# A load that waits for a memset: SyncE issues the second load of wq behind half of GpSimd's zeros

## The chip, the core and the metric

The kernel runs on one core of one Trainium2 chip. The metric is the device time of one execution in microseconds (us); before the change the median of 3 runs is 218.84 us (218.81 to 218.87). Where a profile is read, its times come from one further execution taken with the profiler, and are counted from the start of its span.

## The reference, cut to what matters

One decoding step for two tokens. Attention over the last 4096 positions of a cache and a dense layer with Mish work on the same input, and a sigmoid gate mixes them:

```python
g = sigmoid((x * gate_w).sum(-1, keepdims=True))          # x: 2 x 1 x 512
q = (x @ wq)                                               # 512 x 4096: 32 heads of 128
scores = einsum(q, k[last 4096]) * 128 ** -0.5             # 8 kv heads, each for 4 query heads
a = (softmax(scores) @ v[last 4096]) @ wo                  # 4096 x 512
h = x @ w1 + b1                                            # 512 x 1792
b = (h * tanh(softplus(h))) @ w2                           # 1792 x 512
out = g * a + (1 - g) * b
```

All of it is float32. The weights and the part of the cache that is read are some 91 MB, and each byte is used for only two tokens.

## The kernel before, in words

**Loads.** All large inputs pass through three rotating buffers of 128 partitions x 64 KB (the pool `stream`, lines 61 and 70 to 76). SyncE (SP) issues nearly all loads; its DMAs share one queue, which is spread over 16 DMA engines, so there are 16 rings that each work off their share of a load. The order of issue on SP is: `wq` in two pieces (line 74, called from line 78), the small inputs `sm` (line 80: x, the gate's weights, the bias), eight loads `kv` of 8 MB each, one kv head's keys and values (line 74, called from line 296), `w12` (w1, a part of wo, a part of w2), then the rest of w1, wo and w2 (lines 320, 333, 337). The first piece of `wq`, `in_wqh`, has 2048 columns (HEAD, 1 MB: 8 KB in each partition); the second, `in_wqt`, has the other 14336 (7 MB: 56 KB in each partition). The first two `kv` loads find a buffer free; every later one waits until TensorE is done with the buffer that it takes.

**Work at the start.** GpSimd (POOL) builds an identity matrix and from it small masks (`fold`, `key`, lines 91 to 98), writes ones and zeros (`ones`, `x32`, `qz`, `padded`: lines 103, 106, 109, 112), and when `sm` has landed copies x into `x32` (line 107). `qz`, 128 x 1152, is the tile for the queries: zeros everywhere but where line 155 later puts the transposed queries of each head, so that a matmul of line 163 can take a block of it as weights. ScalarE waits with its first instruction, an activation table load, until the first load has landed (lines 85 to 88). TensorE multiplies x with wq (line 143), so its first instruction needs the first piece of `wq` and `x32`.

**Then**, for each of the 8 kv heads: scores (line 163), maximum, exponential, transposes, values (line 187). Last come w1 (line 258), wo (line 348) and w2 (line 358), the copy of the result (line 391) and the store (line 392).

A scheduler sets the order on each engine. It places an instruction by its own estimates, and what stands on one engine in the program's text is not always the order in which that engine runs it; `keep_in_program_order` (also called `pin`) marks instructions that it leaves in the order of the text.

Of the kernel before, what the change touches and what calls it, by code (L numbers as in the profile page):

```python
# [17 lines left out]
HKV = 8  # L18
# [38 lines left out]
def decode_kernel(ctx: ExitStack, tc: tile.TileContext, res, stored, small, wqh, wqt, kv_in, w12, wo, w2, *rest):  # L57
    *parts, before, behind, out = rest
    nc = tc.nc
# [8 lines left out]
    loads = []  # L68

    def load(name, *parts):  # L70
        t = stream.tile([P, 2 * CHUNK], F32, tag="s", name=name)
        x = 0
        for cols, src in parts:
            loads.append(nc.sync.dma_start(t[:, x : x + cols], src))  # L74
            x += cols
        return t

    wq_t = load("wq", (HEAD, wqh[:, :HEAD]), (2 * CHUNK - HEAD, wqt[:, : 2 * CHUNK - HEAD]))
    sm = const.tile([P, SMALL], F32, name="sm")
    loads.append(nc.sync.dma_start(sm, small))  # L80
    xT = sm[:, : (DC + SLOTS) * B].rearrange("p (c b) -> p c b", b=B)
    gw = sm[:, (DC + SLOTS) * B : (DC + SLOTS) * B + DC]
    b1 = sm[:, (DC + SLOTS) * B + DC :]
# [4 lines left out]
                      reason="ScalarE begins behind the first load")  # L88
# [17 lines left out]
    nc.gpsimd.memset(x32, 0.0)  # L106
    nc.gpsimd.tensor_copy(x32[:, :, ::RS], xT)  # L107
    qz = const.tile([P, HKV, BN * (Q + REP)], F32, name="qz")
    nc.gpsimd.memset(qz, 0.0)
    sizes = (HQ * Q, CUTS[1] * Q, (FC - CUTS[1]) * WIDE, WIDE)  # L110
    padded = const.tile([P, sum(sizes)], F32, name="padded")
    nc.gpsimd.memset(padded, 0.0)
# [182 lines left out]
    for kv in range(HKV):  # L295
        t = load(f"kv{kv}", (2 * CHUNK, kv_in[kv][:, : 2 * CHUNK]))
        p = scores(kv, t[:, :CHUNK])
        ms = tops() if kv == HKV - 1 else None
        pT = turned(kv, p)
        values(kv, pT, t[:, CHUNK:], 0, 1)  # L300
        if kv == HKV - 1:
            kf, kl = factors(ms)
        values(kv, pT, t[:, CHUNK:], 1, 2)
        if kv == HKV - 1:
            r = shares(kl)
        values(kv, pT, t[:, CHUNK:], 2, NT)
    w12_t = load("w12", (AHEAD + CUTS[1] * D, w12))

    def flat(src, cuts, size):
# [4 lines left out]
    x = (WO[-1] - WO[0]) * REP * D  # L314
# [16 lines left out]
    x = 0  # L331
# [3 lines left out]
    x = AHEAD + CUTS[1] * D  # L335
# [31 lines left out]
    first = WO[0] * REP  # L367
# [19 lines left out]
    for ld in loads[-8:]:  # L387
        tc.add_manual_dep(landed.ins, ld.ins.name,
                          mybir.DependencyInfo(mybir.DependencyClass.Sync, mybir.DependencyReason.DATA),
                          reason="SyncE sees the last loads land ahead of the store")  # L390
# [5 lines left out]
                      reason="the store reads the copy")  # L396
# [72 lines left out]
```

## Time and profile before

| | before |
|---|---|
| median of 3 runs | 218.84 us |
| the profiled execution: its own time | 218.95 us |
| the profiled execution: span of its trace | 217.1 us |
| DMA moved, mean over the span | 91.38 MB, 421 GB/s |
| busy: PE, DVE, ACT, POOL | 52%, 10%, 7%, 5% of the span |
| first instruction on PE | 23.12 us |

The span runs from the first instruction in the trace to the last; the 1.85 us by which the execution's own time is longer lie outside it. In the rows a line such as "L74" is a line of the kernel, "SPq" is SyncE issuing DMAs, and names like `wq<-in_wqt` are the tile written and the source. Time after a bar or in brackets as "idle before" is that of the engine just ahead of the instruction, with what ended it.

### The profile page before, as it was taken

What the parts mean: (1) busy time and instruction counts of PE and PEld (TensorE: products, weight loads), DVE (VectorE), ACT (ScalarE), POOL (GpSimd) and SP (SyncE); (2) the same over time, 40 slices, a digit from 0 to 9 for tenths busy, and PEclk for the clock granted to TensorE, in tenths of its full rate; (3) what the DMA queues carried; (4) which work ended last, traced back from release to release, by engine and by line L of the source; (5) the groups of instructions that cost most, each with busy time, mean ns of one, the idle gap of its engine ahead of it and who ended that gap; (6) DMA issues with size and microseconds to landing.
All of it is one profiled execution on the core that took longest, in us unless ns stands there. A gap on an engine that the chain in (4) does not pass through costs nothing.

```text
span 217.1 us, 1858 instructions
## 1 busy us (share of the span) xinstructions
PE 113.3 (52%) x826; PEld 34.5 (16%) x826; DVE 21.5 (10%) x32; ACT 15.4 (7%) x34; POOL 11.4 (5%) x34
## 2 busy tenths in 40 slices
PE   0000797367055609533770753287066608759995
PEld 0000312112011102101120210012011101213342
DVE  0000000010001320100105010010501001250100
ACT  0200001011002000200010020002002000301001
POOL 8000000000000000000000000000000230100300
PEclk9999999889859975996797699679958957999699
DMA  9798998999989998999999999999999999999894
GB/s 362 338 507 351 546 411 386 399 522 423 399 386 519 426 411 386 495 447 399 399 483 450 399 411 447 483 399 411 450 471 399 423 447 430 430 383 468 377 410 159
DMA packets 2752, 91.38 MB, mean 421 GB/s; under 512 B 566, under 2 KB 646, under 8 KB 954
## 3 DMA queue, kind: packets, MB, share of 16 engines
q1 hardware_dynamic: 2602, 91.24, 97.6%
q8 instruction: 6, 0.10, 0.2%
q0 software_dynamic: 144, 0.05, 0.1%
HBM read 91.24 MB, written 0.04 MB: 421 GB/s over the span
## 4 chain that ended last, share of the span: by engine, by line
DMA 78%; PE 15%; ACT 2%; SPq 2%; DVE 1%; issue 1%; POOL 1%; ACTq 0%
DMA kv<-in_kv 61%; DMA w<-in_w 17%; PE sc L163 8%; PE o L187 5%; ACT p L168 1%; PE fin L358 1%; DVE mx L166 1%; SPq L320 1%; PE pp L175 1%; ACT pT L176 1%; POOL wo L316 1%; SPq L333 0%; SPq L74 0%; SPq L80 0%; DVE res L391 0%
## 5 line engine op out<-in xcount | busy, mean ns | idle before, releaser
L163 PE MATMUL sc<-kv,qz 128*32 128x512 f32 x256 | 43.3, 839 | 54.7 <-DMA kv<-in_kv 54.7
L187 PE MATMUL o<-kv,pT 128*32 128x512 f32 x256 | 29.5, 596 | 5.8 <-ACT pT L176 5.8
L163 PEld LDWEIGHTS sc<-kv,qz 128*32 128x32 f32 x256 | 9.7, 149 | 87.7 <-DMA kv<-in_kv 61.3
L143 PE MATMUL qp<-wq,x 128*32 128x512 f32 x64 | 11.4, 760 | 23.1 <-POOL x L107 23.1
L166 DVE TENSOR_REDUCE mx<-sc 128x1 f32<-128x512 f32 x8 | 5.5, 692 | 112.3 <-PE sc L163 112.3
L168 ACT ACTIVATE p<-sc,mx 128x512 f32<-128x512 f32 x8 | 5.5, 687 | 131.2 <-DVE mx L166 131.2
L175 PE MATMUL pp<-ident,p 128*128 128x128 f32 x32 | 5.2, 286 | 12.1 <-ACT p L168 12.1
L187 PEld LDWEIGHTS o<-kv,pT 128*32 128x32 f32 x256 | 7.3, 109 | 20.9 <-issue 13.2
L316 POOL MEMSET wo<- 128x1536 f32 x1 | 1.4, 1377 | 144.4 <-PE o L187 144.4
L197 DVE TENSOR_REDUCE od<-om 128x256 f32<-128x1024 f32 x4 | 7.6, 1898 | 0.1
L143 PEld LDWEIGHTS qp<-wq,x 128*32 128x32 f32 x64 | 2.4, 134 | 28.7 <-POOL x L107 23.1
L348 PE MATMUL acc<-wo,padded 128*32 128x512 f32 x56 | 6.9, 593 | 0.0
L194 DVE TENSOR_TENSOR om<-o,pick 128x1024 f32<-128x1024 f32 x4 | 4.9, 1225 | 19.3 <-PE o L187 19.3
L175 PEld LDWEIGHTS pp<-ident,p 128*128 128x128 f32 x32 | 3.4, 140 | 18.6 <-ACT p L168 18.6
L176 ACT COPY pT<-pp 128x512 f32<-128x512 f32 x8 | 4.7, 585 | 6.2 <-PE pp L175 6.2
L258 PE MATMUL hp<-w,x 128*32 128x512 f32 (+1 forms) x30 | 3.6, 540 | 2.5 <-DMA w<-in_w 2.5
L348 PE MATMUL acc<-w,padded 128*32 128x512 f32 x22 | 4.3, 896 | 0.4 <-DVE padded L241 0.4
L348 PEld LDWEIGHTS acc<-wo,padded 128*32 128x32 f32 x56 | 2.5, 109 | 3.5 <-issue 2.5
L258 PE MATMUL hp<-wo,x 128*32 128x512 f32 x6 | 2.7, 592 | 0.0
L132 DVE RECIPROCAL g<-g 128x2 f32<-128x2 f32 x1 | 0.2, 165 | 22.4 <-POOL g L131 22.4
L358 PE MATMUL fin<-w,padded 128*32 128x128 f32 x56 | 2.1, 277 | 0.4 <-DMA w<-in_w 0.4
L149 PE MATMUL qt<-ident,qs 128*128 128x128 f32 x8 | 1.3, 286 | 1.4 <-ACT qs L146 1.4
(71 smaller groups left out, 35.8 us busy)
## 6 DMA issues: line engine op xcount, KB each, us to landing
wq<-in_wqt SPq DMA_DIRECT2D x1, 7168.0 KB, 21.5
w<-in_w SPq DMA_DIRECT2D x1, 6144.0 KB, 41.3
wo<-in_wo SPq DMA_DIRECT2D x1, 5120.0 KB, 29.6
wo<-in_wo SPq DMA_DIRECT2D x1, 2048.0 KB, 34.1
wq<-in_wqh SPq DMA_DIRECT2D x1, 1024.0 KB, 4.9
w<-in_w SPq DMA_DIRECT2D x1, 1024.0 KB, 36.0
w<-in_w SPq DMA_DIRECT2D x1, 512.0 KB, 35.4
w<-in_w SPq DMA_DIRECT2D x1, 256.0 KB, 21.1
```

Of the source, the lines that this page charges most:

```text
L143: nc.tensor.matmul(qp[Q * k : Q * k + Q, :], x32[:, c, :], w[:, c, k, :], start=(c == 0), stop=(c == DC - 1))
L163: nc.tensor.matmul(sc[Q * j : Q * j + Q, :], qz[:, kv, m * Q : m * Q + Q], t[:, (m * NJ + j) * 512 : (m * NJ + j + 1) * 512], start=(m == ...
L166: nc.vector.tensor_reduce(mx[:, kv : kv + 1], sc, axis=AX.X, op=ALU.max, negate=True)
L168: nc.scalar.activation(p, sc, AF.Exp, bias=mx[:, kv : kv + 1], accum_out=ls[:, kv : kv + 1])
L175: pin(nc.tensor.transpose(pp[:, c, :], p[:, c * P : (c + 1) * P], ident))
L176: nc.scalar.copy(pT, pp)
L187: pin(nc.tensor.matmul(o[Q * j : Q * j + Q], pT[:, c, Q * j : Q * j + Q], t[:, (c * NJ + j) * 512 : (c * NJ + j + 1) * 512], start=(c == 0 ...
L194: nc.vector.tensor_tensor(ov, pair[0].rearrange("p k (m d) -> p k m d", m=BN), pick[:, None, :, None].to_broadcast([P, 2, BN, DH]), op=ALU ...
L197: nc.vector.tensor_reduce(od[:, kv - 1 : kv + 1], ov.rearrange("p k m d -> p k d m"), axis=AX.X, op=ALU.add)
L258: nc.tensor.matmul(hp[Q * j : Q * j + Q, :n], x32[:, c, :], w[:, :n], start=(c == 0), stop=(c == (DC + SLOTS if j in away else DC) - 1))
L348: return nc.tensor.matmul(acc[Q * j : Q * j + Q, :], lhsT, rhs, start=(n_col[j] == 1), stop=(n_col[j] == n))
L358: nc.tensor.matmul(fin[Q * j : Q * j + Q, :], lhsT[:, y : y + Q], rhs[:, j * P : (j + 1) * P], start=(done[0] == 0), stop=(done[0] == n_fi ...
```

## The change

Three things change in the text. The loads of `wq`, `kv` and `sm` are marked to stay in program order. The memset of `qz` becomes two, each of half the heads (128 x 576). And SyncE's issue of `loads[1]`, which is `in_wqt`, the second piece of `wq`, depends on the first of these two memsets: a semaphore from GpSimd. `DependencyReason.DATA` is only the kind of the entry; the load reads nothing that the memset writes.

```diff
         for cols, src in parts:
-            loads.append(nc.sync.dma_start(t[:, x : x + cols], src))
+            loads.append(tc.keep_in_program_order(nc.sync.dma_start(t[:, x : x + cols], src)))
             x += cols
...
-    loads.append(nc.sync.dma_start(sm, small))
+    loads.append(tc.keep_in_program_order(nc.sync.dma_start(sm, small)))
...
     qz = const.tile([P, HKV, BN * (Q + REP)], F32, name="qz")
-    nc.gpsimd.memset(qz, 0.0)
+    half = nc.gpsimd.memset(qz[:, : HKV // 2], 0.0)
+    tc.add_manual_dep(loads[1].ins, half.ins.name,
+                      mybir.DependencyInfo(mybir.DependencyClass.Sync, mybir.DependencyReason.DATA),
+                      reason="the first load has the queues for itself at first")
+    nc.gpsimd.memset(qz[:, HKV // 2 :], 0.0)
     sizes = (HQ * Q, CUTS[1] * Q, (FC - CUTS[1]) * WIDE, WIDE)
```

Line numbers behind the change are 4 higher. On SyncE, at the program's start, the DMAs stood so (tile, source, shape; a number behind a name is that of the buffer, and brackets name the engine whose semaphore the instruction waits for):

```order
L74 DMA wq<-in_wqh 128x2048
L74 DMA wq<-in_wqt 128x14336
L80 DMA sm<-in_small 128x32
L74 DMA kv_170<-in_kv 128x16384
L74 DMA kv_216<-in_kv 128x16384
```

And now, in the same place:

```order
L74 DMA wq<-in_wqh 128x2048
L74 DMA wq<-in_wqt 128x14336 [waits Pool_49]
L80 DMA sm<-in_small 128x32
L74 DMA kv_171<-in_kv 128x16384
L74 DMA kv_217<-in_kv 128x16384
```

The order is the same; the second DMA has got a wait for GpSimd, and the three behind it stand behind that wait. On GpSimd, from the zeros of `x32` on, the order was:

```order
L106 MEMSET x_94 128x224
L93 TENSOR_TENSOR fold<-ident 128x32 [waits Pool_49]
L109 MEMSET qz 128x1152
L95 TENSOR_TENSOR fold<-fold,ident 128x32 [waits Pool_49]
L112 MEMSET padded 128x1744
L95 TENSOR_TENSOR fold<-fold,ident 128x32 [waits Pool_49]
L98 TENSOR_TENSOR key<-fold 128x8 [waits Pool_49]
L117 COPY padded<-fold 128x2
```

And now:

```order
L106 MEMSET x_94 128x224
L93 TENSOR_TENSOR fold<-ident 128x32 [waits Pool_49]
L109 MEMSET qz 128x576
L95 TENSOR_TENSOR fold<-fold,ident 128x32 [waits Pool_49]
L113 MEMSET qz 128x576
L95 TENSOR_TENSOR fold<-fold,ident 128x32 [waits Pool_49]
L116 MEMSET padded 128x1744
L98 TENSOR_TENSOR key<-fold 128x8 [waits Pool_49]
L121 COPY padded<-fold 128x2 [waits Pool_49]
```

The first half stands where the whole memset stood, the second half behind the next addition of `fold`, and the zeros of `padded` have moved behind the second of those additions. Every other engine has the same instructions in the same order as before.

## Prediction

> **What bounds the kernel now.** I read the page first, its row of DMA queues and its chain of work that ended last:
>
> ```profile
> q1 hardware_dynamic: 2602, 91.24, 97.6%
> DMA 78%; PE 15%; ACT 2%; SPq 2%; DVE 1%; issue 1%; POOL 1%; ACTq 0%
> ```
>
> The queue that carries SyncE's loads keeps its 16 rings busy for 97.6% of the span, and 78% of the chain is DMA. So the time is that of 91 MB through 16 rings, plus a stretch ahead of the first byte and one behind the last. An edit to the order of issue can matter in two ways only: by what it does to the rings' throughput, and by a stretch in which a ring has nothing to do. Both are looked for at the start, so next the timeline, its SP and POOL rows of the first microseconds (start, duration, engine, line), with the first row of PE:
>
> ```profile
> 0.73 0.39 SPq L74 DMA_DIRECT2D wq<-in_wqh  x1
> 1.17 0.41 SPq L74 DMA_DIRECT2D wq<-in_wqt  x1
> 1.35 0.27 POOL L106 MEMSET x<- 128x224 f32 x1
> 1.62 0.43 SPq L80 DMA_DIRECT2D sm<-in_small  x1
> 1.79 1.05 POOL L109 MEMSET qz<- 128x1152 f32 x1
> 2.10 1.29 SPq L74 DMA_DIRECT2D kv<-in_kv  x2
> 3.00 1.54 POOL L112 MEMSET padded<- 128x1744 f32 x1
> 22.86 0.21 POOL L107 COPY x<-sm 128x14 f32<-128x14 f32 x1 [17.70 <-DMA sm<-in_small]
> 23.12 1.92 PE L143 MATMUL qp<-wq,x 128*32 128x512 f32 x2 [23.12 <-POOL x L107]
> ```
>
> SyncE issues five loads without a pause, from 0.73 to 3.39 us. TensorE starts only at 23.12, since `sm` sits in the rings behind all of `wq`; nobody but ScalarE's table load uses the first piece early. Third, the DMA view of the window 0 to 6 us, 40 slices of 0.15 us:
>
> ```profile
> GB/s 0 0 0 0 0 0 0 0 0 0 0 382 55 0 164 218 218 218 109 546 273 492 382 437 437 437 437 437 437 382 1475 382 983 2294 1529 382 0 0 0 0
> ```
>
> A packet is evidently counted whole where it starts (2294 GB/s is over five times the mean of 421), which helps here: the pieces can be told apart. Slice 12 (1.65 to 1.80) holds the first packets, 0.92 to 1.07 us after the issue at 0.73. From 3.45 on the rate is even. The jump at slice 31 (4.50 to 4.65) is the first of the far larger packets of `in_wqt`, and the last of them start in slice 36 (5.25 to 5.40). So each ring goes over from the first piece to the second at some point between 4.50 and 5.40, and what it needs of the second piece before that is only that it be queued.
>
> The last stretch, by windows (length, busy time of five engines, granted clock, DMA share, GB/s), and the chain's last pieces:
>
> ```profile
> 212.50:213.00 0.50, 0.09 (x7) 0.10 (x8) 0.00 (x0) 0.40 (x1) 0.00 (x0) 1.00 0.97 393
> 213.00:213.50 0.50, 0.50 (x21) 0.50 (x25) 0.00 (x0) 0.19 (x1) 0.00 (x0) 1.00 0.76 303
> 213.50:214.00 0.50, 0.50 (x28) 0.46 (x19) 0.00 (x0) 0.00 (x0) 0.00 (x0) 1.00 0.63 242
> 214.00:214.40 0.40, 0.40 (x22) 0.31 (x16) 0.00 (x0) 0.00 (x0) 0.00 (x0) 1.00 0.15 56
> ...
> 176.77 36.03 DMA w<-in_w
> 212.80 0.14 issue
> 212.93 2.26 PE fin L358 x64
> ```
>
> The rings do not end together: the DMA share falls from 0.97 to 0.15 over the 1.4 us before 214.4. What the start gives or takes reaches the end only on the rings that are last there.
>
> **The change part by part.** The time is worked out against the profiled execution: span 217.1 us and 1.85 us around it, 218.95 us in all, 0.11 us above the median of the three runs, 218.84.
>
> *When the second load is issued.* The first half is 576 elements in each partition. The rows for 224 and 1152 elements (0.27 and 1.05 us) give 0.84 ns for an element, so the half takes 0.27 + 352 x 0.00084 = 0.57 us. It starts where the whole one did, at 1.79, and ends at 2.36. How fast SyncE reacts to GpSimd shows later in the chain, where a load waits for a memset in the same way:
>
> ```profile
> 172.22 1.39 POOL wo L316
> 173.61 0.02 issue
> 173.62 0.89 SPq L320
> ```
>
> So 0.02 us more: the second load is issued at 2.38 instead of 1.17, which is 1.21 us later. Queued behind the wait on SyncE are `sm` (1.62 to about 2.83) and two `kv` (2.10 and on to about 3.31 and on, ending near 4.60). Nobody waits for these: in the rings they lie behind `wq`, which has landed only here (KB, us from issue to landing):
>
> ```profile
> wq<-in_wqt SPq DMA_DIRECT2D x1, 7168.0 KB, 21.5
> wq<-in_wqh SPq DMA_DIRECT2D x1, 1024.0 KB, 4.9
> ```
>
> that is at 1.17 + 21.5 = 22.7 us, 18 us after the last delayed issue. With that cover gone each microsecond of delay would cost a microsecond.
>
> *Does a ring run dry?* The second piece's first packets are ready 0.92 to 1.07 us behind the issue, as for the first piece: at 3.30 to 3.45. For the slowest ring I have a bound only: the first load is at 546 GB/s in slice 20, which ends at 3.00, so by then the rings have their work, 2.27 us after the issue. That gives 4.65 at the latest. Needed are the packets between 4.50 and 5.40. On the likely value there is over 1 us of room; on the bound the earliest ring waits 0.15 us and one in the middle none. I take 0, with 0.15 as the end on the side of a loss; it is nearer to 0, since a ring slow to get its first piece is also the one that is done with it late.
>
> The Trainium skill, "DMA: Bandwidth & Descriptors", section "Rules for kernel authors", says to issue a DMA early so that its fixed setup lies beside other work, and this change does the contrary. By it alone the 1.21 us would be a loss. Here the row of slices leaves 1 us of setup covered by the 2.9 us and more between the first packets and the first change-over, so the trace supports no loss as long as that cover holds.
>
> *What the first load can gain.* From 1.65 to 3.45 the twelve slices sum to 3057, times 0.15 us: 459 KB. The window behind them shows what the same load does once it runs:
>
> ```profile
> 3.45:4.50 1.05, 0.00 (x0) 0.00 (x0) 0.00 (x0) 0.00 (x0) 1.05 (x1) 1.00 1.02 429
> ```
>
> At 429 GB/s these bytes take 1.07 of the 1.80 us, so the slow start costs 0.73 us, and that is the most that the change can bring. The least is 0, if the slowness is that of a first access, or of the rings' own start. For a gain speaks that the slow slices, 1.80 to 2.85, are those in which SyncE pushes the second load, `sm` and the first `kv`. Against it: the second `kv` is issued up to 3.39, while the four slices from 2.85 to 3.45 already average 423. And the one later place where several loads are issued beside a full stream, six DMAs of SyncE and three of GpSimd from 173.6 to 177.3, shows no loss against the window behind it:
>
> ```profile
> 173.60:177.30 3.70, 0.00 (x0) 0.00 (x0) 0.00 (x0) 0.00 (x0) 1.86 (x3) 0.63 1.03 443
> 177.30:185.00 7.70, 5.23 (x33) 1.24 (x33) 0.69 (x1) 0.52 (x1) 0.00 (x0) 0.73 0.96 412
> ```
>
> That also prices the four moved issues, which now fall into the first load's steady stretch: 443 against 412 says nothing is lost. I take 0 for the gain as well, as this later row is a direct view of issues beside a stream, and keep 0.73 as the other end.
>
> The Trainium skill, "Perfetto Trace Analysis", section "DMA Instruction — HWDGE (DVE, Sync)", has the issuing sequencer hold the descriptor generator for itself until all descriptors of its DMA are made, and only then go on. By it the first load's descriptors are complete at 0.73 + 0.39 = 1.12, ahead of the second issue at 1.17; there would be nothing to disturb and the gain would be 0. The trace has the two issues apart in that way, and does not show the descriptors.
>
> *GpSimd.* Two halves take 2 x 0.57 = 1.14 us instead of 1.05, so 0.09 us more. GpSimd then idles 17.70 us until `sm` lands; this cover hides it, and without it the cost would be 0.09. The moved zeros of `padded` and the additions of `fold` lie under the same cover. Marking loads to stay in order changes nothing on SyncE.
>
> The sum is 0 + 0 + 0: 218.95 for an execution like the profiled one, and 218.8 as a median.
>
> **The rivals.** *The first load does start faster, and the whole stream with it.* Then the slices from 1.80 to 2.85 fill up. Half of the 0.73 us, since the first access itself cannot be free, gives 218.84 − 0.37 = 218.5, all of it 218.1. Against a gain in full: the windows at the end show a last ring alone for a while; rings that gain unevenly bring only what the last one gains, down to nothing.
>
> *The rings run dry between the two pieces: slower.* The place is the change-over, 4.50 to 5.40. It decides once SyncE issues the second load later than 4.50 − 1.07 = 3.43 us with the likely setup, or later than 2.23 with the longest. GpSimd's durations are the uncertain piece: should the half take as long as the whole did, 1.05 us, the issue is at 2.86, and with the longest setup the packets are there at 5.13, so the earliest ring stands still for 0.63 us. If that is one that ends last, the time is 218.84 + 0.63 = 219.5; with a ring that changes over midway, at 4.95, 0.18: 219.0. A price in between is 219.3. It needs the long end of both, hence unlikely.
>
> **How the numbers follow.** About 0.2%, 0.44 us, is what a measurement of this kernel can tell from no change. No change that can be told: chance 0.50, at 218.8, its own range 218.4 to 219.2. A faster start: 0.35, between 218.1 and 218.7, four fifths of it below 218.40. Dry rings: 0.15, between 219.0 and 219.5, most of it beyond 219.28. Faster by over 0.2% then has 0.28, within 0.2% 0.60, slower 0.12. The range 218.1 to 219.2 takes in the first two cases and the lower half of the third.
>
> **What would show it.** Right: `in_wqt` issued near 2.38; slow slices up to 2.85 as before; the large packets starting in 4.50 to 5.40; `sm` landing and PE's first row near 23.1; the same fall of the DMA share around 214. If the slices behind 1.80 fill up and the large packets start earlier than 4.50, with PE's first row earlier by as much, the second case has come about. Zeros in the slices between 4.4 and 5.6 with PE's first row later are the third. PE's first row shifted but the end not, or the reverse, would say that my single line from start to end is wrong.

## The result, and the profile after

| | before | after |
|---|---|---|
| median | 218.82 us (4 runs, 218.78 to 218.87) | 219.78 us (4 runs, 219.66 to 220.37) |
| ratio after/before | | 1.0049, 95% interval 1.003 to 1.0067 |
| the profiled execution: its time, span | 218.95, 217.1 us | 219.66, 217.8 us |

The change makes the kernel 0.96 us slower, outside the range of the prediction (218.1 to 219.2) and on the side to which I had given 0.12. The profiled executions differ by 0.71 us, 0.7 of it in the span.

The timeline's start (start, duration, engine, line) went as worked out: the half memset takes 0.57 us, and the second load is issued at 2.39 instead of 1.17:

```profile
0.73 0.39 SPq L74 DMA_DIRECT2D wq<-in_wqh  x1
1.79 0.57 POOL L109 MEMSET qz<- 128x576 f32 x1
2.39 0.33 SPq L74 DMA_DIRECT2D wq<-in_wqt  x1
2.76 0.43 SPq L80 DMA_DIRECT2D sm<-in_small  x1
3.24 0.91 SPq L74 DMA_DIRECT2D kv<-in_kv  x2
23.38 0.20 POOL L107 COPY x<-sm 128x14 f32<-128x14 f32 x1 [18.31 <-DMA sm<-in_small]
```

`sm`, which lies behind all of `wq` in the rings, is used at 23.38 instead of 22.86, so half a microsecond is gone by then. The DMA view of 0 to 6 us, slices of 0.15 us, looks for it around the first load:

```profile
GB/s 0 0 0 0 0 0 0 0 0 0 0 437 164 0 0 273 109 164 546 328 492 328 492 273 546 328 492 382 492 328 492 983 3168 1529 382 382 0 0 0 0
```

The slow slices from 1.80 to 2.70 are still there. From 1.65 to 3.45 the slices sum to 3333 instead of 3057, 41 KB more, and the window behind them has lost 24 KB of that again:

```profile
3.45:4.50 1.05, 0.00 (x0) 0.00 (x0) 0.05 (x1) 0.00 (x0) 1.05 (x1) 1.00 0.97 406
```

So the first load gains 17 KB by 4.50, or 0.04 us. The large packets of the second load start from 4.65 to 5.40, and no slice between is empty: in this view the rings do not run dry. What has become slow is the second load's own packets. The view of 0 to 12 us (slices of 0.3 us) shows where, before and then after:

```profile
GB/s 0 0 0 0 0 191 27 191 218 328 382 410 437 437 410 928 1639 956 0 0 0 0 382 1720 573 382 0 0 0 382 1147 1147 382 0 0 0 382 956 1338 382
```

```profile
GB/s 0 0 0 0 0 218 82 137 137 437 410 382 437 437 410 737 2349 382 0 0 0 0 0 1529 765 382 382 0 0 0 382 1911 191 573 0 0 0 382 1911 191
```

Each hump is the moment at which the rings start one further packet of 56 KB. Before, the humps start in slices 16, 23, 30 and 37, seven slices or 2.1 us apart. After, the second one starts in slice 24 and drags on to slice 27, and the third starts in 31: some first packets take 0.3 us longer and more. From the third hump on the distance is seven slices again.

The traces also keep every single packet with its start and its length, and these records give the sizes. On a ring the next packet starts as the last one ends, so the rings can be told apart. A packet of 56 KB usually takes 2.12 us. The second load's first packet takes longer, as a mean over the 16 rings by 0.07 us in before and by 0.28 us in after (at most by 0.35 and 0.79). The second packet takes 0.01 and 0.08 us longer, and from the third on it is 0.02 us at most. One ring of after also stands idle for 0.18 us, until 2.90 us behind the issue. The rings then end the second load 0.28 us later on average (22.26 instead of 21.98) and the last of them 0.49 us later (22.82 instead of 22.33), which is the half microsecond by which `sm` is late.

The rate of a longer window is no measure of this, since its edge can cut a hump. Up to 20.00 us it is 420 GB/s in before and 401 in after; up to 21.00 us it is 412 in both (before and after in turn; last columns: DMA share, GB/s):

```profile
5.40:20.00 14.60, 0.00 (x0) 0.00 (x0) 0.00 (x0) 1.28 (x1) 0.00 (x0) 1.00 0.97 420
5.40:20.00 14.60, 0.00 (x0) 0.00 (x0) 0.00 (x0) 1.28 (x1) 0.00 (x0) 1.00 0.93 401
5.40:21.00 15.60, 0.00 (x0) 0.00 (x0) 0.00 (x0) 1.28 (x1) 0.00 (x0) 1.00 0.95 412
5.40:21.00 15.60, 0.00 (x0) 0.00 (x0) 0.00 (x0) 1.28 (x1) 0.00 (x0) 1.00 0.96 412
```

The end follows, by the last pieces of the chain and the windows of after:

```profile
176.09 37.38 DMA w<-in_w
213.48 0.14 issue
213.61 2.29 PE fin L362 x64
```

```profile
213.50:214.00 0.50, 0.39 (x16) 0.42 (x20) 0.00 (x0) 0.14 (x1) 0.00 (x0) 1.00 0.64 254
214.00:214.40 0.40, 0.40 (x24) 0.40 (x17) 0.00 (x0) 0.00 (x0) 0.00 (x0) 1.00 0.37 143
214.40:215.00 0.60, 0.60 (x28) 0.45 (x23) 0.00 (x0) 0.00 (x0) 0.00 (x0) 1.00 0.16 61
```

The last wait for w2 ends at 213.48 instead of 212.80, and the rings are busy up to 215 where they had ended by 214.4. By the packet records, 64 short packets mark the ends of the last four loads on the 16 rings; their mean is 0.20 us later than in before, and the last of them 0.72 us later (215.08 instead of 214.36). So the mean lateness of the rings is only a part of the loss, and the rest lies on the rings that end last. How it gathers on them is not shown.

### The profile page after: what moved, and what is told of

It reads as the page before. It is cut to its first block, busy times and chain, and to the rows that moved or that the text cites. A ratio compares the mean times of both kernels' runs of the same rounds, so it can differ in the third digit from the quotient of the medians.

```text
span 217.8 us, 1859 instructions
## 1 busy us (share of the span) xinstructions
PE 118.0 (54%) x826; PEld 35.4 (16%) x826; DVE 21.6 (10%) x32; ACT 15.5 (7%) x34; POOL 11.4 (5%) x35
## 4 chain that ended last, share of the span: by engine, by line
DMA 77%; PE 16%; ACT 2%; SPq 2%; POOL 1%; DVE 1%; issue 1%; ACTq 0%; POOLq 0%
DMA kv<-in_kv 60%; DMA w<-in_w 17%; PE sc L167 8%; PE o L191 6%; ACT p L172 1%; PE fin L362 1%; DVE mx L170 1%; SPq L324 1%; PE pp L179 1%; ACT pT L180 1%; POOL wo L320 1%; SPq L337 0%; POOL qz L109 0%; SPq L80 0%; DVE res L395 0%
## 5 line engine op out<-in xcount | busy, mean ns | idle before, releaser
L167 PE MATMUL sc<-kv,qz 128*32 128x512 f32 x256 | 45.5, 877 | 51.0 <-DMA kv<-in_kv 51.0
L191 PE MATMUL o<-kv,pT 128*32 128x512 f32 x256 | 31.1, 622 | 5.8 <-ACT pT L180 5.8
L147 PE MATMUL qp<-wq,x 128*32 128x512 f32 x64 | 11.9, 794 | 23.6 <-POOL x L107 23.6
L167 PEld LDWEIGHTS sc<-kv,qz 128*32 128x32 f32 x256 | 10.2, 153 | 85.3 <-DMA kv<-in_kv 57.6
```

The lines of the kernel that those rows point to most:

```text
L147: nc.tensor.matmul(qp[Q * k : Q * k + Q, :], x32[:, c, :], w[:, c, k, :], start=(c == 0), stop=(c == DC - 1))
L167: nc.tensor.matmul(sc[Q * j : Q * j + Q, :], qz[:, kv, m * Q : m * Q + Q], t[:, (m * NJ + j) * 512 : (m * NJ + j + 1) * 512], start=(m == ...
L191: pin(nc.tensor.matmul(o[Q * j : Q * j + Q], pT[:, c, Q * j : Q * j + Q], t[:, (c * NJ + j) * 512 : (c * NJ + j + 1) * 512], start=(c == 0 ...
```

## Experiments

They ran on several chips. Each is compared with the kernel before on its own chip, and "loss" below is the difference of these two medians. "Issue" is that of the second load on SyncE. "Lead" is from there to the middle of the change-over to the second load, 4.95 us with HEAD 2048, near 6.45 with HEAD 3072 and near 7.6 with HEAD 4096. "Long by" is read from the packet records of the profiled execution: by how much the second load's first packet, as a mean over the 16 rings, takes longer than the load's packets usually do (2.12 us for 56 KB, 1.97 for the 52 KB of HEAD 3072, 1.82 for the 48 KB of HEAD 4096). In before it is 0.07 us.

| run | issue, us | lead, us | median, us | loss, us | ratio, 95% interval | long by, us |
|---|---|---|---|---|---|---|
| split_only | 1.18 | 3.8 | 218.89 | 0.01 | 0.9997 to 1.0016 | 0.00 |
| wait_x32 | 1.66 | 3.3 | 218.88 | 0.00 | 0.9995 to 1.0014 | 0.01 |
| wait_sum0 | 1.87 | 3.1 | 218.93 | 0.09 | 0.9999 to 1.0018 | 0.07 |
| after_again, after_third | 2.38, 2.39 | 2.6 | 219.82, 219.69 | 0.96, 0.80 | 1.0039 to 1.0066, 1.0031 to 1.0055 | 0.48, 0.23 |
| wait_sum1 | 2.60 | 2.4 | 219.58 | 0.74 | 1.0023 to 1.0049 | 0.30 |
| wait_whole | 2.87 | 2.1 | 219.45 | 0.58 | 1.0017 to 1.0036 | 0.16 |
| wait_second_half, second_half_again | 3.11 | 1.8 | 218.98, 218.94 | 0.10, 0.05 | 1.0001 to 1.002, 0.9995 to 1.0012 | 0.16, 0.12 |
| wait_padded | 4.81 | 0.1 | 220.67 | 1.81 | 1.0069 to 1.0097 | 0.67 |
| small_waits | 1.18 | 3.8 | 218.91 | 0.03 | 0.9993 to 1.0012 | 0.00 |
| kv_waits | 1.17 | 3.8 | 218.90 | 0.01 | 0.9991 to 1.0009 | 0.01 |
| small_held | 2.39 | 2.6 | 219.75 | 0.86 | 1.0029 to 1.0064 | 0.18 |
| head4096 | 1.18 | 6.4 | 219.05 | 0.21 | 1.0004 to 1.0025 | 0.00 |
| head4096_wait | 2.39 | 5.2 | 218.93 | 0.09 | 0.9995 to 1.0014 | 0.00 |
| head4096_late | 4.82 | 2.8 | 219.97 | 1.10 | 1.0038 to 1.0067 | 0.34 |
| head4096_later | 5.66 | 1.9 | 219.79 | 0.94 | 1.0032 to 1.0068 | 0.20 |
| head3072_wait | 2.39 | 4.1 | 219.30 | 0.43 | 1.0013 to 1.0037 | 0.00 |

**Which part of the change, and how late.** Three theories: LATE (the second load is slow if it is issued too shortly ahead of its turn), BEHIND (the loads pushed behind it disturb it), PHASE (a first load that runs alone brings the rings in step).

split_only takes the wait away:

```diff
-    tc.add_manual_dep(loads[1].ins, half.ins.name,
-                      mybir.DependencyInfo(mybir.DependencyClass.Sync, mybir.DependencyReason.DATA),
-                      reason="the first load has the queues for itself at first")
```

> The two half memsets and the marked order stay, the wait is gone. All three theories put the loss on the wait: the time is that of before, 218.8 us, and the first row of PE is near 23.1 us. Over 219.2 would mean that the memsets or the marks cost something themselves.

218.89 against 218.88: the halved memset and the marked order cost nothing. The whole loss is the wait's.

wait_x32 waits for an earlier instruction:

```diff
-    tc.add_manual_dep(loads[1].ins, half.ins.name,
+    tc.add_manual_dep(loads[1].ins, early.ins.name,    # early = nc.gpsimd.memset(x32, 0.0)
```

> The second load waits for the zeros of x32 instead, so it is issued near 1.65 us, about 0.5 us later than before and 0.75 earlier than in the changed kernel. Theory LATE (the second load's packets are slow at first since it is issued too shortly ahead of the change-over from the first piece to the second): little or nothing, 218.8 to 219.1. Theory BEHIND (the small load and the two kv loads, pushed later, disturb the second load's first packets): issues end near 3.9, a part of the loss, 219.0 to 219.5. Theory PHASE (with the first load alone, the rings run in closer step and get in each other's way at the change-over): half of the slow stretch is cleared, 219.0 to 219.5.

No loss, against BEHIND and PHASE, and the second load's packets have their usual length. Each hump of the view of 0 to 12 us is two or three slices wide:

```profile
GB/s 0 0 0 0 0 191 137 109 191 355 382 437 382 437 437 573 2540 382 0 0 0 0 191 2294 573 0 0 0 0 191 2294 573 0 0 0 0 0 2485 573 0
```

small_waits leaves the second load alone and holds what is behind it:

```diff
-    tc.add_manual_dep(loads[1].ins, half.ins.name,
+    tc.add_manual_dep(loads[2].ins, half.ins.name,
```

> The second load is issued at once as in before (1.17 us); the wait for the half memset is on the small load behind it, so that load and the two kv loads are issued as late as in the changed kernel. LATE: as before, 218.8, PE's first row near 23.1. BEHIND: the whole loss, 219.5 to 220.0, PE's first row near 23.6. PHASE: as before or close, 218.7 to 219.0.

`sm` is issued at 2.39 and the `kv` loads from 2.76, and there is no loss: against BEHIND, for LATE and PHASE.

wait_second_half waits for the second half memset in place of the first:

```diff
-    tc.add_manual_dep(loads[1].ins, half.ins.name,
+    tc.add_manual_dep(loads[1].ins, whole.ins.name,    # whole = nc.gpsimd.memset(qz[:, HKV // 2 :], 0.0)
```

> The second load waits for the second half of the zeros: issue near 3.1 us, 0.7 later than in the changed kernel and still ahead of 3.43, from where the rings would run dry with a setup of 1.07 us. LATE: worse than the changed kernel by about the 0.7 us of delay, 220.2 to 220.7. BEHIND: the later issues fall fully on the second load's first packets, 219.8 to 220.5. PHASE: the first load is just as much alone as in the changed kernel, so the same loss, 219.6 to 220.0.

All three miss: 0.7 us later than the change, and a loss of 0.10. This run also settles the other half of the question. Its first load is alone in the rings until the second's packets can be there near 4.1, and the DMA view of 0 to 6 us is

```profile
GB/s 0 0 0 0 0 0 0 0 0 0 0 382 164 55 164 218 55 55 328 437 328 492 382 437 437 382 492 382 328 546 328 1202 1639 2349 1147 382 0 0 0 0
```

The twelve slices from 1.65 sum to 3060, against 3057 before. The first load starts as slowly with nothing queued behind it, so nothing is gained by holding others back.

**Is the loss there again, and what does a dry ring cost.** after_again is the changed kernel once more. wait_padded waits for `late = nc.gpsimd.memset(padded, 0.0)`.

> The changed kernel as it is, once more. The longer wait for the second half cost under 0.1 us at the median though PE's first row came 0.7 us later, so LATE, BEHIND and PHASE can't stand as they were put. Theory SPREAD (issuing the second load shortly ahead of its turn makes its first packets slow by an amount that changes from run to run, and most often the end does not see it; the first four runs lay high): median 218.9 to 219.3, single runs from 218.8 to 220.4. Theory OWN (the issue at 2.39 us in particular does harm, by what is under way just then): median 219.6 to 220.0 again.

> The second load waits for the zeros of padded, issue near 4.8 us: its packets can't be there before 5.7, and the rings want them from 4.5 on, so the rings run dry by 0.5 to 1.2 us. Price of a dry stretch. If the end follows the start by a microsecond for a microsecond: 219.4 to 220.1. If the tail of the kernel hides a part of it, as with the wait for the second half: 218.9 to 219.4, with PE's first row 0.8 to 2 us later all the same.

The loss is there again, 0.96 us: OWN, not SPREAD. wait_padded loses 1.81 us, above both expectations. Its DMA view of 0 to 6 us shows the dry stretch:

```profile
GB/s 1 0 0 0 0 0 0 0 0 0 0 382 164 55 55 164 0 273 492 382 492 328 492 382 437 382 492 328 546 273 492 273 109 0 0 0 0 0 1911 1147
```

The first large packets start in slice 39 (5.70 to 5.85), 0.89 to 1.04 us behind the issue at 4.81, as the prediction had the setup. That is eight slices or 1.2 us later than in before. The rest, 0.6 us, is a slow second load on top of the dry stretch: its first packets take 0.67 us longer than usual, 0.60 us more than in before. Every ring has its first large packet by 1.68 us behind the issue.

**All on one chip.** Theories CHIP (the chip decides), PUSH (the descriptors of the `kv` loads reach the rings at the change-over), COLD (a load issued shortly ahead of its turn is slow at first, whatever else is issued). after_third and second_half_again are repeats; the other two move the loads behind:

```diff
 small_held: the changed kernel, and the small load waits for the zeros of padded
+    tc.add_manual_dep(loads[2].ins, late.ins.name,
 kv_waits: no wait on the second load, the first kv load waits for the second half
+            tc.add_manual_dep(loads[3].ins, whole.ins.name,
```

> The changed kernel beside the other three of this call, on one chip. It lost 0.5% twice, 219.78 and 219.82 us, while the wait for the second half was measured on another chip and lost nothing. Theory CHIP (the chip decides whether a late second load costs something): this and the wait for the second half move together here. Theories PUSH and COLD (below): 219.6 to 220.0 again.

> The second load waits for the second half of the zeros, once more. CHIP: the same loss as the changed kernel, or both none. PUSH (the descriptors of the kv loads, issued 3.2 to 4.1 us in the changed kernel, reach the rings about 1 us later, at the change-over, and slow its packets): here they are issued at 4.0 to 4.9 and come behind most of it, 218.8 to 219.1. COLD (a load issued only shortly ahead of its turn is slow in its first packets, whatever else is issued): more than the changed kernel, 219.8 to 220.3.

> The second load waits for the half as in the changed kernel (2.39 us); the small load waits for the zeros of padded as well, so that it and the two kv loads are issued only from 4.8 us on, up to 6. They are not wanted before 22.7. PUSH: the change-over is free of their descriptors, so the loss is gone or moved, 218.8 to 219.2. COLD: the loss stays, 219.6 to 220.0.

> The second load and the small one are issued at once as in before; the two kv loads wait for the second half of the zeros, so they are issued from 3.1 to 4.0 us, nearly as in the changed kernel (3.2 to 4.1). PUSH: the loss is there without any wait on the second load, 219.4 to 219.9. COLD: none, 218.8 to 219.0.

On one chip the changed kernel loses 0.80 and the wait for the second half 0.05: CHIP falls. small_held loses 0.86 though SyncE issues nothing but the second load between 2.4 and 4.8, and kv_waits loses nothing though the `kv` loads are issued at 3.11: PUSH falls. The views of 0 to 12 us show the second load's packets in small_held, where the second hump spreads over three slices with a straggler in slice 29, and in kv_waits, where it has two:

```profile
GB/s 0 0 0 0 0 164 109 109 137 382 437 437 437 437 410 601 2704 0 191 0 0 0 0 1338 1147 382 0 0 191 0 1147 1338 382 0 0 191 0 765 1720 382
```

```profile
GB/s 0 0 0 0 0 137 82 164 109 355 437 437 437 410 437 382 2212 956 0 0 0 0 0 2103 956 0 0 0 0 0 1911 1147 0 0 0 0 0 1911 1147 0
```

The first packets are long by 0.23 us (after_third) and 0.18 us (small_held) where the time is lost, by 0.12 us (second_half_again) and 0.01 us (kv_waits) where it is not. The harm is in the second load's own packets, and comes from when that load itself is issued. COLD is half right: right for small_held and kv_waits, wrong for the wait for the second half.

**Lead or moment.** HEAD is changed (2048 to 4096 or 3072), which moves the second load's turn, and the wait goes to the first and second addition of `fold` (`sums[0]`, `sums[1]`) or to the unsplit memset of `qz` (wait_whole).

> The kernel before with HEAD 4096: the first piece has 2 MB, the second 6 MB, the issues are as before (1.17 us). Control for the next run. The rings go over to the second piece near 7.5 us instead of near 5. No theory sees a loss: 218.7 to 219.1.

> The changed kernel with HEAD 4096: the second load is issued at 2.39 us, but its turn comes near 7.5, so the lead is 5 us instead of 2.6. Theory LEAD (the harm comes from the time between the issue and the turn): as its control, 218.7 to 219.1, and no slow packets behind the change-over. Theory WINDOW (the harm comes from the moment of issue, whatever the turn): 0.6 to 1.0 us over its control.

> The second load waits for the first addition of fold, issue near 1.86 us, between the wait for x32 (1.66, no loss) and the changed kernel (2.39, loss 0.9). LEAD: a loss that grows with the time of issue, 219.0 to 219.3. WINDOW: none if the harmful moment begins later, 218.8 to 219.0, or all of it, 219.6 to 219.9.

> The second load waits for the second addition of fold, issue near 2.6 us, between the changed kernel (2.39, loss 0.9) and the wait for the second half (3.11, loss under 0.1). LEAD: at least the changed kernel's loss, 219.7 to 220.1. WINDOW: a value between, 219.0 to 219.8, which says how sharply the loss ends.

The changed kernel's issue at 2.39 costs nothing once the turn is at 7.6: less than its control, within the noise of both. That speaks for the lead and against the moment. The other two runs do not: 218.93 (wait_sum0) and 219.58 (wait_sum1) lie in the ranges of WINDOW and just below those of LEAD, so LEAD was not yet settled. With a lead of 3.1 (wait_sum0) nothing measurable is lost; with 2.4 (wait_sum1) it is 0.74, and the second hump of its view of 0 to 12 us drags over six slices, 24 to 29. No ring of wait_sum1 stands idle at the change-over, so a standstill is not what costs the time:

```profile
GB/s 0 0 0 0 0 191 55 218 27 382 437 410 437 410 382 410 2048 956 191 0 0 0 0 956 573 956 191 191 191 0 191 956 1338 191 191 191 0 0 956 1147
```

> The zeros of the queries are one memset again and the second load waits for all of it, issue near 2.86 us: between the second addition (2.60, loss 0.74) and the second half (3.11, loss under 0.1). Whether the loss falls off gradually or at a step: gradually 219.2 to 219.4, with the step still to come 219.6 to 219.8, behind it 218.9 to 219.0.

> HEAD 4096 with the wait for the zeros of padded: issue near 4.81 us, turn near 7.5, so nearly the lead of the changed kernel (2.6 to 2.7 us), but well behind the start-up of the first load. LEAD (the time between issue and turn decides): a loss of 0.6 to 1.0 against HEAD 4096 without a late issue, 219.5 to 220.0, with slow packets behind 7.5. START (the issue does harm only near the end of the rings' slow start, and when the turn follows soon): none, 218.8 to 219.2.

> The changed kernel with HEAD 3072: issue at 2.39 us, turn near 6.2, lead 3.8. LEAD and START: with the longer lead the loss is smaller than the changed kernel's, 218.9 to 219.4. If it is as large, 219.6 to 219.9, then something between this and HEAD 4096 decides.

wait_whole loses 0.58, between its neighbours and between two of the ranges that were expected. head4096_late is the decisive one. Its issue, at 4.82, lies two microseconds behind the slow start of the first load, and with nearly the changed kernel's lead it loses about the same, 1.10, or 0.92 against the median of its control head4096. Its first packets are long by 0.34 us, and the second ones by 0.25; in head4096_wait (lead 5.2) and in the control none is long.

The control has a weakness: HEAD 4096 costs something without any long packet. Its median is 0.21 us above before, and its profiled execution took 220.07 us. head3072_wait had no control with HEAD 3072, and its first packets have their usual length, so its 0.43 says nothing of the lead.

**The dip.** The loss falls with the lead from 2.6 to 2.1 and is nearly gone at 1.8. head4096_later has that lead at another moment; it waits for one further memset, 128 x 768 of `od`, which is overwritten later.

```diff
+    late = nc.gpsimd.memset(od[:, :6], 0.0)
+    tc.add_manual_dep(loads[1].ins, late.ins.name,
```

> HEAD 4096, and the second load waits for a further memset (768 elements of a tile that is written later anyway), issue near 5.65 us, turn near 7.6: a lead of 1.9 us, as with the wait for the second half (3.11, turn 5.0), which lost under 0.1 us while leads of 2.1 to 2.6 lost 0.6 to 0.9. HEAD 4096 with a lead of 2.7 lost 1.1. If the lead alone sets the loss, its dip at 1.9 included: 218.9 to 219.2. If any lead under 3 us costs, and the dip belongs to the moment 3.11: 219.5 to 220.2.

It loses 0.94 against before on its chip; the control of HEAD 4096, measured on another chip, accounts for some 0.21 of it. So leads from 1.9 to 2.8 cost 0.6 to 1.1 us against before in this kernel at two places, and the wait until 3.11 is an exception (two chips, 10 and 11 runs).

The packet records narrow the exception. Its first packets are long as well, by 0.16 and 0.12 us, as in wait_whole (0.16, loss 0.58); only the end does not show it. In wait_second_half one ring ends the second load at 23.02, later than any ring of after (22.82), but the mean of the rings is 0.08 us behind that of before, and the last end mark comes at 214.27, with 214.36 in before. Why the end shows the long packets of wait_whole and not these stays open. No version tried beats the kernel before.

## Why the prediction was wrong, point by point

*When the second load is issued*: right. 2.39 against 2.38, the half memset 0.57 us as worked out, and the loads behind it are not missed: kv_waits and small_waits show that holding them costs 0.01 and 0.03 us.

*What the first load can gain*: right with 0, and for a better reason than the one given. With the second load kept away until 3.11 the slow slices are as before (3060 against 3057), so what is queued behind the first load does not make them slow.

*GpSimd, and the marks*: right, 0.01 us by split_only.

*Does a ring run dry?* This is the step that failed. It said that what a ring "needs of the second piece before that is only that it be queued", took the 0.92 to 1.07 us from an issue to its first packets as the whole setup, and so found over 1 us of room. For rings with nothing else to do the setup was sized rightly: wait_padded has its first packets 0.89 to 1.04 behind the issue and the last ring's at 1.68, inside the bound of 2.27. But to be queued in time is not enough for full speed. With leads of 2.1 to 2.6 us the first packet of the second load is 0.16 to 0.48 us longer than usual as a mean over the rings, and the loss is 0.6 to 1.0 us; with leads above 3 it is 0.07 us at most. The sum had 0 for this term. The bound of 2.27 us for the slowest ring did not hold either: the idle ring of after got its first packet 2.90 us behind the issue, and one of after_again 3.59 us. The prediction watched for empty slices, and the loss came as longer packets.

*The rival that was slower* had the right sign and place, the change-over, and the wrong mechanism: it priced a standstill of 0.63 us at most, under two unlikely conditions. Single rings did stand idle (0.18 us in after, 0.90 and 0.77 on the worst ring of after_again and after_third), but one does so for 0.17 us in split_only and kv_waits too, which lose nothing, and wait_sum1 loses 0.74 without one. *That the rings with the last work set the end* held: the last end mark of after is 0.72 us later, the mean of the marks 0.20. But PE's first row is not a measure of it: wait_second_half has `sm` used at 23.56, later than the changed kernel, and hardly loses.

The rule of the Trainium skill, "DMA: Bandwidth & Descriptors", section "Rules for kernel authors", to issue a DMA early and overlap its fixed setup, was on the right side, and I set it aside because the setup that the trace shows, 1 us, was covered. The runs bear out that an early issue is better, and want a larger lead than that setup: 3 us here. What the rings do with such a lead, and why packets that start in time are slow without it, no run here shows.

## What to carry to other kernels

Where the loads' queue is the bound, a wait put into the issuing engine can cost long before the queue runs dry: here a lead of 3.1 us cost nothing that could be told, and one of 2.6 us cost 0.8 to 1.0 us. Empty slices show a dry queue only, and the rate of a long window depends on where its edge cuts the packets: compare how far the packets behind the change-over lie apart. Only the second load of this kernel was tried; whether later loads need the same lead is not shown. And before holding a transfer back for another's sake, look whether the other is any quicker alone.

## What was not expected of the hardware

- The first packets of a load whose issue leads its turn by 1.8 to 2.8 us are long, though most rings have their packet in time: by 0.12 to 0.48 us over the usual 2.12 us (0.20 and 0.34 over 1.82 with HEAD 4096), against 0.07 at most with leads above 3. From the third packet on they have nearly their usual length.
- The first load's slow microsecond, 0.73 us lost by 3.45, is there even when nothing else is queued.
- A ring that has other work can get a new load's first packet late: 2.90 us behind the issue in after and 3.59 us in after_again, while in wait_padded, where all 16 rings stood idle, each had it by 1.68 us.
- The exception at 3.11 us (losses 0.10 and 0.05) is reproducible and unexplained.
